# Seventy narrow warm-up products and forty one-element memsets in a hand-ordered linear-attention and MLP kernel

## The chip, the core and the metric

The kernel runs on one core of a Trainium2 chip. The metric is the device time of one execution in microseconds (us); the median of the runs is what counts. Five engines work side by side, each on its own queue, in order: TensorE (PE for its products, PEld for its weight loads), VectorE (DVE), ScalarE (ACT), GpSimd (POOL), and SyncE (SP), whose queue issues every data transfer here. Semaphores tie them together.

## The reference, cut to what matters

Sizes: 2048 rows, 512 columns, 32 heads of 16, an inner width of 1792 in the MLP; all tensors are bf16.

```python
def _layernorm(x, eps=1e-5):
    return (x - mean(x)) / sqrt(var(x) + eps)

def _A_ref(x, wqkv, wo):                      # linear attention
    q, k, v = heads(x @ wqkv)
    phi = lambda t: where(t > 0, t + 1, exp(t)) + 1e-6
    pq, pk = phi(q), phi(k)
    kv = einsum("bhsd,bhse->bhde", pk, v)
    z = einsum("bhsd->bhd", pk)
    num = einsum("bhqd,bhde->bhqe", pq, kv)
    den = einsum("bhqd,bhd->bhq", pq, z)[..., None] + 1e-6
    return merge(num / den) @ wo

def _B_ref(x, w1, w2):                        # MLP
    return maximum(x @ w1, 0) @ w2

h  = x + _A_ref(_layernorm(x), A_wqkv, A_wo)
h2 = h + _B_ref(_layernorm(h), B_w1, B_w2)
```

## The kernel before

The 2048 rows are 16 tiles of 128 rows; four tiles make a chunk. Every step is a small function `op_NAME`, and one string, `ORDER`, lists the calls: a word such as `K.3.7` calls `op_K(3, 7)`, the first number being the tile or chunk and the others banks of the accumulator `bk` (eight banks) or slices. Nothing else schedules: the order of the words is the order of the instructions on each engine, and semaphore waits are derived from the data. An engine's queue is in order, so a word that waits holds up all that stands behind it on the same engine.

The head of the program, on which the prediction rests, works tile by tile:

- `lx.t.n`, `lk`, `lq` load rows of x and the weights of k and q, on SP. `const` sets small constants on VectorE (and `zeros`, which lies in `m_sb`), and the identity on GpSimd.
- `S.t` and `A.t` (VectorE) take the statistics of a tile and join them in `mv`; `R.t.n` (ScalarE) makes `rstd` by a Ln and an Exp, two activations; `N.t` (VectorE) writes the normalised tile into `h_nat`.
- `T.t.b` transposes a tile on TensorE, in four products with the identity; `E.t` (ScalarE) copies the result to `lnT`. Later tiles go by `X.t` instead, a transposing transfer on SP.
- `K.t.b` makes the k projection, four products of 512 columns; `F`, `U`, `M`, `D` (or `W`) turn it into phi(k) on ScalarE and VectorE, in `eb` and `rb`; `G.t` adds k times x into four banks.
- `table` loads the one ScalarE table that holds both Ln and Exp. Where an activation stands in the order before a table that has its function, the build puts a table load ahead of it.
- `warm` and `warmf` are products of zeros into a bank that is not yet in use: `warm.n.b` has 512 columns of bf16, `warmf.n.b` 256 columns of f32.

Then follow the q projection (`Q`, `qF` and so on), the state `kv` and its product with `wo`, in `m_sb` (`m`), the denominators (`dn`, `dnl`, `dnx`), which are transposed into `rd` by SP (`dt`) and multiplied in by `dm` (into `pqs`), the attention output with the residual (`h`, `hD`), the second layernorm (`s`, `a`, `r`, `n`, and `x` or `t` for the transposes), and the MLP: `p` with relu in `pA` or `pD`, then `f`, `fo` and the store `fd`. The last tile's `f` comes in three pieces of 128, 256 and 128 columns.

Of the kernel before, what the change touches and what calls it, by code (L numbers as in the profile page):

```python
# [15 lines left out]


ORDER = """
const lx.0.1 lx.1.1 warmf.4.3 warm.1.3 S.0 table A.0 R.0.1 S.1 lx.2.2 lk.0.2 warm.1.3 N.0 A.1 S.2 R.1.1 lk.2.2
lx.4.2 A.2 T.0.7 E.0 warm.1.3 S.3 R.2.1 K.0.1.0.2 lx.6.2 A.3 R.3.1 K.0.1.2.2 N.1 T.1.5 F.0.1 E.1 N.2 N.3 T.3.2  # L20
lx.8.4 E.3 S.4 S.5 A.4 T.2.5 lx.12.4 lq.0.2 A.5 K.1.0.0.2 R.4.2 S.6 M.0.1 N.5 S.7 N.4 X.5 E.2 U.0.1 D.0.1 K.3.7
K.1.0.2.2 F.3.1 M.3.1 X.4 K.2.3.0.2 U.3.1 A.7 A.6 K.2.3.2.2 U.1.1 R.6.2 F.2.1 F.1.1 G.0 D.3.1 G.3 S.9 U.2.1 N.7
N.6 S.8 K.5.1 K.4.0 M.2.1 A.8 A.9 R.8.2 U.4.2 M.1.1 X.7 D.2.1 F.4.2 D.1.1 N.9 S.12 X.6 N.8 X.9 G.2 K.7.3 S.13
A.12 A.13 G.1 R.12.2 K.6.2 K.9.1 M.4.2 S.10 F.6.2 N.12 D.4.2 S.11 A.10 U.6.2 X.8 M.6.2 N.13 G.4 X.12 K.8.0 A.11
R.10.2 S.14 D.6.2 G.5 G.6 X.13 N.10 N.11 S.15 F.8.2 M.8.2 X.11 A.15 U.8.2 A.14 D.8.2 R.14.2 G.7 za.2 za.4 K.12.0
G.9 K.13.1 N.15 N.14 X.10 lq.2.2 K.11.3 F.12.2 K.10.2 M.12.2 U.12.2 F.10.2 masks X.15 X.14 lv.0.2 lv.2.2 l1.0.2
U.10.2 za.6 D.12.2 M.10.2 G.8 za.8 D.10.2 Q.0.1.1 Q.0.0.0 qF.0.0.2 qU.0.0.2 za.10 G.12 K.14.2 K.15.3 Q.0.2.0
za.12 Q.0.3.1 G.13 F.14.2 G.11 qF.0.2.2 l2.10.4 qM.0.0.2 M.14.2 W.14.2 zf.12 G.10 qD.0.0.2 qM.0.2.2 G.14
qU.0.2.2 lo.0.2 z.3.1.14 z.2.1.14 G.15 z.1.1.14 z.0.1.14 qD.0.2.2 zc gA.0.2 gA.2.2 Q.1.0.2 zh dn.0.1 Q.1.1.3
dnl.0 kv.2.7 lo.2.2 kv.1.7 kv.3.7 dnx.0.2.2 qF.1.0.2 kv.0.7 l2.3.4 dnx.0.0.2 Q.1.2.0 l1.2.2 rt.2.6 kx qM.1.0.2  # L30
Q.1.3.1 qF.1.2.2 m.0.4 m.1.5 rv.2 Q.3.1.7 qW.1.0.2 m.3.6 Q.2.3.2 dt.3 qM.1.2.2 mA.0.2 qW.1.2.2 dt.0 dt.1 m.2.5
Q.2.1.4 dn.1.0 mA.2.2 dm.0.0.2 Q.2.2.1 dm.0.2.2 dnl.1 dnx.1.2.2 h.3.6 dnx.1.0.2 h.1.5 rt.6.3 hD.3 qF.2.2.2 dt.7
s.3 re.6 h.0.0 dt.4 qU.2.2.2 hD.1 dt.5 a.3 hD.0 s.1 s.0 a.1 qM.2.2.2 a.0 Q.3.0.6 Q.2.0.3 n.3 h.2.5 n.0 dm.1.0.2
Q.3.3.1 x.3 dm.1.2.2 qF.3.0.2 hD.2 n.1 s.2 Q.3.2.0 qU.2.0.2 qF.2.0.2 h.5.2 h.6.3 a.2 qU.3.0.2 qM.2.0.2 h.4.7 n.2
qF.3.2.2 x.0 qD.2.0.2 t.2.5 qD.2.2.2 hD.4 x.1 hD.6 h.7.4 dn.2.6 hD.5 hD.7 e.2 dnl.2 qM.3.0.2 p.0.0.5 dnx.2.2.2
p.0.13.7 p.0.1.6 p.0.8.2 p.0.9.3 dnx.2.0.2 qD.3.0.2 s.4 l2.7.3 p.0.11.4 pA.0.0.2 dt.11 l2.0.3 dt.9 dt.10 r.0.4
qM.3.2.2 qW.3.2.2 s.6 dt.8 p.0.12.6 s.7 pD.0.12.2 p.0.3.1 p.0.2.0 pA.0.8.2 dn.3.2 p.0.5.7 dnl.3 p.0.4.6 a.7
dm.2.0.2 pA.0.2.2 dnx.3.0.2 dnx.3.2.2 dm.2.2.2 pD.0.4.2 h.9.0 h.8.5 p.0.6.6 p.0.7.7 dt.13 dt.12 s.5 dt.14
p.0.10.3 hD.8 dt.15 s.8 a.6 pD.0.6.2 a.4 pA.0.10.2 n.6 f.1.1.0.7 hD.9 n.7 f.1.1.7.7 s.9 dm.3.0.2 dm.3.2.2 h.11.7
a.5 n.5 h.12.2 h.15.6 h.14.4 fo.1 h.10.5 hD.11 f.0.7.0.7 hD.12 x.6 a.8 h.13.1 a.9 f.3.3.0.7 f.3.3.7.7 x.7 hD.15  # L40
n.4 hD.14 f.0.7.7.7 x.4 f.2.0.0.7 hD.13 fo.3 x.5 p.1.0.6 s.12 s.11 n.8 hD.10 fo.0 p.1.1.7 a.11 fd.0 p.1.5.3 s.10
pD.1.0.2 f.2.0.7.7 a.12 n.12 n.9 s.14 p.1.4.2 n.11 p.1.8.4 fo.2 p.1.3.1 r.4.4 a.10 a.14 p.1.13.7 p.1.2.0
pD.1.4.2 n.10 x.10 x.11 s.13 p.1.7.2 p.1.9.5 p.1.12.6 a.13 pD.1.2.2 s.15 a.15 pD.1.8.2 n.14 pD.1.12.2 p.1.6.1
n.15 x.9 x.8 pA.1.6.2 f.7.0.0.7 p.1.10.4 fd.1 p.1.11.5 pD.1.10.2 fd.3 f.5.2.0.7 p.2.9.7 p.2.11.5 f.7.0.7.7
f.5.2.7.7 fo.7 p.2.8.6 p.2.10.4 p.2.5.1 pD.2.10.2 p.2.4.0 r.8.4 pA.2.8.2 f.4.4.0.7 fo.5 p.2.2.5 fd.2 pA.2.4.2
p.2.3.6 n.13 f.4.4.7.7 p.2.1.3 x.12 p.2.0.2 f.6.0.0.7 x.14 pA.2.2.2 fo.4 x.13 x.15 p.3.3.7 p.3.7.5 p.3.2.6
r.12.4 p.3.9.4 f.6.0.7.7 pA.2.0.2 p.3.11.1 p.3.8.3 p.3.4.2 fd.4 fd.5 fo.6 pA.3.8.2 pD.3.2.2 p.3.10.0 p.3.5.3
p.3.6.4 pA.3.10.2 fd.7 pA.3.6.2 p.2.6.6 pD.3.4.2 p.2.7.7 pD.2.6.2 p.3.13.5 p.3.1.1 fd.6 p.2.12.6 p.3.0.0
p.2.13.7 f.11.3.0.7 p.3.12.4 pD.2.12.2 f.9.6.0.7 f.9.6.7.7 f.10.7.0.7 pA.3.12.2 pA.3.0.2 f.11.3.7.7 f.10.7.7.7
f.8.2.0.7 f.12.1.0.7 f.8.2.7.7 f.14.5.0.7 f.13.4.0.7 f.15.0.0.14.3.1 f.14.5.7.7 fo.11 fo.9 fo.10 fd.10 fd.11  # L50
fo.15.3.1 fo.8 f.12.1.7.7 fd.9 f.13.4.7.7 fd.8 f.15.0.0.14.0.2 fo.14 fo.12 fd.12 fo.13 fd.15.3.1 fo.15.0.2
f.15.5.0.14.2.1 fd.13 fd.14 fd.15.0.2 fo.15.2.1 fd.15.2.1
"""


# [1 line left out]
def kernel(  # L57
# [155 lines left out]
    def op_warm(n, b):
        for _ in range(n):
            nc.tensor.matmul(bk[:, b, :], lhsT=zeros[:, 0:P], rhs=zeros, start=True, stop=True)
# [376 lines left out]
```

## Time and profile before

| | |
|---|---|
| median of 3 runs | 170.3 us (169.92 to 170.45) |
| profiled execution, first to last instruction | 168.8 us |
| instructions | 2286 |
| TensorE busy | 163.1 us, 97% of the span |
| VectorE busy | 104.4 us, 62% |
| ScalarE busy | 65.1 us, 39% |
| transfers | 15.49 MB, of them 41 transposes on SP |

The page of the profile gives times of one execution. A busy share counts the time in which at least one instruction of the engine ran; products overlap in TensorE's pipeline, so a row of products is longer than their pitch, and small waits between products don't show in the share. The chain of work that ended last, in order of time, shows which engine the end waited for. A few records of products are missing from the trace; each leaves a gap of 0.05 us called "issue". Line numbers such as L310 are those of the kernel before.

### The profile page before, as it was taken

How to read it: one execution, taken by the hardware profiler on the slowest of the kernel's cores; microseconds unless marked ns; L12 is line 12 of the kernel's file. 1: busy time of each engine (PE TensorE's matmuls, PEld its weight loads, DVE VectorE, ACT ScalarE, POOL GpSimd, SP SyncE). 2: the span in 40 equal slices, each digit the busy share in tenths (PEclk: the TensorE clock that was granted, in tenths of full speed). 3: DMA queues.
4: the chain of work that ended last, by engine and by line, in shares of the span. 5: the costliest groups of instructions: out<-in, count | busy, mean ns of one | idle time of the engine just before them, and what ended most of it. 6: DMA issues, size and time to landing. Idle time of an engine off the chain costs nothing.

```text
span 168.8 us, 2286 instructions
## 1 busy us (share of the span) xinstructions
PE 163.1 (97%) x855; PEld 78.0 (46%) x871; DVE 104.4 (62%) x205; ACT 65.1 (39%) x97; POOL 4.8 (3%) x21
## 2 busy tenths in 40 slices
PE   7989999999999999999999999999999999999993
PEld 5344344445644454444444444444444444444553
DVE  3899998997668999699819879215102432050251
ACT  3698775875879947432000003004320420400000
POOL 7400000000000000000000000000000000000000
PEclk9999999999999999999999999999999999999999
DMA  4975575689533353534130015500320000002023
GB/s 112 352 245 97 97 66 124 176 270 378 174 64 65 77 138 87 134 62 95 37 62 0 31 31 122 126 4 0 62 93 0 31 0 4 0 0 93 0 65 94
DMA packets 30491, 15.49 MB, mean 92 GB/s; under 512 B 23184, under 2 KB 29328, under 8 KB 30480
## 3 DMA queue, kind: packets, MB, share of 16 engines
q1 hardware_dynamic: 30480, 15.34, 35.5%
q8 instruction: 7, 0.11, 0.3%
q14 instruction: 4, 0.03, 0.1%
HBM read 7.86 MB, written 2.10 MB: 59 GB/s over the span
## 4 chain that ended last, share of the span: by engine, by line
PE 85%; DVE 7%; DMA 4%; issue 1%; SPq 0%
PE bk L541 29%; PE bk L521 28%; PE bk L505 8%; PE bk L318 8%; PE bk L362 6%; PE bk L310 4%; DVE st L237 3%; DMA x_nat<-in_A_x_dram 2%; DMA lnT<-h_nat 2%; DVE h_nat L262 2%; PE bk L459 1%; DVE eb L335 1%; PE bk L403 1%; PE bk L415 1%; SPq L201 0%
## 5 line engine op out<-in xcount | busy, mean ns | idle before, releaser
L541 PE MATMUL bk<-w_sb,at 128*128 128x512 bf16 (+2 forms) x247 | 50.1, 355 | 0.3
L521 PE MATMUL bk<-lnT,w_sb 128*128 128x512 bf16 x219 | 50.0, 379 | 0.3
L527 ACT ACTIVATE at<-bk 128x1024 bf16<-128x1024 f32 x14 | 14.2, 1023 | 57.4 <-PE bk L521 57.4
L541 PEld LDWEIGHTS <-at 128*128 128x128 bf16 x252 | 23.6, 98 | 25.4 <-ACT at L527 0.3
L549 DVE SCALAR_TENSOR_TENSOR gT<-bk,rstd,h_nat 128x512 bf16<-128x512 f32 (+2 forms) x18 | 12.2, 689 | 35.7 <-PE bk L541 35.6
L521 PEld LDWEIGHTS <-w_sb 128*128 128x128 bf16 x224 | 21.8, 98 | 25.8
L532 DVE TENSOR_SCALAR at<-bk 128x1024 bf16<-128x1024 f32 x14 | 17.1, 1218 | 12.8 <-PE bk L521 12.6
L328 ACT ACTIVATE eb<-bk 128x1024 bf16<-128x1024 f32 (+1 forms) x18 | 16.6, 928 | 6.6 <-PE bk L310 4.8
L310 PE MATMUL bk<-wk_sb,lnT 128*128 128x512 bf16 x63 | 15.3, 380 | 0.4 <-ACT lnT L291 0.3
L505 PE MATMUL bk<-m_sb,pqs 128*128 128x512 bf16 x63 | 15.4, 380 | 0.1
L318 PE MATMUL bk<-lnT,wq_sb 128*128 128x512 bf16 x61 | 15.1, 379 | 0.1
L362 PE MATMUL bk<-at,h_nat 128*128 128x512 bf16 x55 | 13.5, 379 | 0.1
L331 ACT ACTIVATE rb<-bk 128x1024 bf16<-128x1024 f32 (+1 forms) x14 | 12.5, 904 | 0.3 <-PE bk L310 0.3
L511 DVE TENSOR_TENSOR h_nat<-bk,x_nat 128x512 bf16<-128x512 f32 x16 | 10.5, 680 | 2.9 <-PE bk L505 2.9
L237 DVE BATCH_NORM_STATS2 st<-x_nat 128x6 f32<-128x512 bf16 x16 | 10.8, 680 | 2.4 <-DMA x_nat<-in_A_x_dram 2.4
L239 DVE BATCH_NORM_STATS2 st<-h_nat 128x6 f32<-128x512 bf16 x16 | 10.7, 683 | 0.1
L310 PEld LDWEIGHTS <-lnT 128*128 128x128 bf16 x64 | 6.0, 98 | 8.4 <-ACT lnT L291 1.0
L362 PEld LDWEIGHTS <-h_nat 128*128 128x128 bf16 x64 | 6.2, 98 | 7.4 <-issue 0.2
L505 PEld LDWEIGHTS <-pqs 128*128 128x128 bf16 x64 | 5.9, 98 | 7.9 <-DVE pqs L495 1.8
L318 PEld LDWEIGHTS <-wq_sb 128*128 128x128 bf16 x64 | 5.9, 98 | 6.4
L472 ACT ACTIVATE wk_sb<-ld 128x1024 bf16<-128x1024 f32 x8 | 8.1, 1050 | 0.1
L335 DVE TENSOR_SCALAR eb<-eb 128x1024 bf16<-128x1024 bf16 (+1 forms) x18 | 6.8, 383 | 0.9 <-ACT eb L328 0.9
(63 smaller groups left out, 93.5 us busy)
## 6 DMA issues: line engine op xcount, KB each, us to landing
out_dram<-gT SPq DMA_DIRECT2D x15, 128.0 KB, 1.9
w_sb<-in_B_w_dram SPq DMA_DIRECT2D x2, 896.0 KB, 9.8
x_nat<-in_A_x_dram SPq DMA_DIRECT2D x2, 512.0 KB, 6.3
w_sb<-in_B_w_dram SPq DMA_DIRECT2D x2, 512.0 KB, 9.5
x_nat<-in_A_x_dram SPq DMA_DIRECT2D x3, 256.0 KB, 4.6
w_sb<-in_B_w_dram SPq DMA_DIRECT2D x2, 384.0 KB, 3.5
wk_sb<-in_A_wqkv_dram SPq DMA_DIRECT2D x2, 256.0 KB, 4.3
wq_sb<-in_A_wqkv_dram SPq DMA_DIRECT2D x2, 256.0 KB, 4.9
```

The lines of the kernel that those rows point to most:

```text
L237: op_S = lambda t: nc.vector.bn_stats(out=st[:, t, :], in_=x_nat[:, t, :])
L310: nc.tensor.matmul(bk[:, b, :], lhsT=lnT[c][:, kd, j * P : (j + 1) * P], rhs=wk_sb[:, kd, :], start=(kd == 0), stop=(kd == KD - 1),)
L318: nc.tensor.matmul(bk[:, b, :], lhsT=wq_sb[:, kd, j * P : (j + 1) * P], rhs=lnT[c][:, kd, :], start=(kd == 0), stop=(kd == KD - 1),)
L328: nc.scalar.activation(out=buf(eb, kind, i, n), in_=bank(at_bank[kind, i], n), func=ACT.Exp)
L331: nc.scalar.activation(out=buf(rb, kind, i, n), in_=bank(at_bank[kind, i], n), func=ACT.Relu)
L362: nc.tensor.matmul(bk[:, KD + kd, :], lhsT=ln_nat[:, t, kd * P : (kd + 1) * P], rhs=pk(t)[:, 0, :], start=(t == 0), stop=(t == NT - 1),)
L505: nc.tensor.matmul(bk[:, b, :], lhsT=pqs[:, (c * KD + jb) % NQ, j * P : (j + 1) * P], rhs=m_sb[:, jb, :], start=(jb == 0), stop=(jb == KD ...
L521: nc.tensor.matmul(bk[:, b, cols], lhsT=w1_sb[:, kd, f * P : (f + 1) * P], rhs=lnT[c][:, kd, cols], start=(kd == 0), stop=(kd == KD - 1),)
L527: nc.scalar.activation(out=acts[c % 2][:, f : f + n, :], in_=bank(at_bank["p", c, f], n), func=ACT.Relu)
L532: nc.vector.tensor_scalar(out=acts[c % 2][:, f : f + n, :], in0=bank(at_bank["p", c, f], n), scalar1=0.0, scalar2=None, op0=ALU.max,)
L541: nc.tensor.matmul(bk[:, b, 0 : w * P], lhsT=acts[c % 2][:, f, j * P : (j + 1) * P], rhs=w2_sb[:, f, k * P : (k + w) * P], start=(f == 0), ...
L549: nc.vector.scalar_tensor_tensor(out=o_t[:, t % NO, cols], in0=bk[:, at_bank["f", t, k], 0 : w * P], scalar=rstd2[:, t : t + 1], in1=h_nat ...
```

## The change

`op_warms` stood in the file unused; it is now called with 70 products of 64 columns, in place of `warmf.4.3` and beside three wide `warm` products. A new `op_idle(n)` writes n memsets of one element on VectorE, all into the same new tile `pad`: 24 of them stand between the statistics of tiles 0 and 1, and 16 between those of tiles 2 and 3. `ORDER` is written anew from its first to its last word, with other banks; all other steps are called as often as before. Two lines of it and the new code:

```diff
-const lx.0.1 lx.1.1 warmf.4.3 warm.1.3 S.0 table A.0 R.0.1 S.1 lx.2.2 lk.0.2 warm.1.3 N.0 A.1 S.2 R.1.1 lk.2.2
-lx.4.2 A.2 T.0.7 E.0 warm.1.3 S.3 R.2.1 K.0.1.0.2 lx.6.2 A.3 R.3.1 K.0.1.2.2 N.1 T.1.5 F.0.1 E.1 N.2 N.3 T.3.2
+lx.0.1 lx.1.1 lx.2.2 lk.0.2 lk.2.2 lx.4.2 lx.6.2 lx.8.4 const S.0 idle.24 S.1 A.0 R.0.1 A.1 N.0 S.2 A.2 warms.70.7
+idle.8 idle.8 S.3 A.3 warm.1.6 table R.1.1 N.1 R.2.1 R.3.1 N.2 N.3 S.4 S.5 A.4 A.5 T.0.1 warm.1.3 warm.1.4 T.1.5 T.2.3
+T.3.2 E.0 E.1 E.3 E.2 K.0.4.0.2 K.0.4.2.2 K.3.0 K.2.2.0.2 K.1.3.0.2 K.2.2.2.2 K.1.3.2.2 S.6 R.4.2 N.5 F.0.1 U.0.1
...
     eps5 = const.tile([P, 1], F32, name="eps5")
+    pad = const.tile([P, 1], F32, name="pad")
...
+    def op_idle(n):
+        for _ in range(n):
+            nc.vector.memset(pad[:], 0.0)
+
     def op_warm(n, b):
         for _ in range(n):
             nc.tensor.matmul(bk[:, b, :], lhsT=zeros[:, 0:P], rhs=zeros, start=True, stop=True)
...
     def op_warms(n, b):
         for _ in range(n):
             nc.tensor.matmul(bk[:, b, 0:64], lhsT=zeros[:, 0:P], rhs=zeros[:, 0:64], start=True, stop=True)
```

The ten loads at the head of SP's queue stand as before. The two loads of `w2` that stood among the `dt` and `x` transposes now follow the other weight loads.

What this makes of the queues is seen at two places. The first is ScalarE's queue from its start to the first copies into `lnT`. Before:

```order
L166 ACT_TABLE_LOAD
L243 ACTIVATE rstd<-mv,eps_73 128x1
L244 ACTIVATE rstd<-rstd 128x1
L243 ACTIVATE rstd<-mv,eps_73 128x1
L244 ACTIVATE rstd<-rstd 128x1
L291 ACTIVATE lnT_81<-bk 128x4x128
```

And now, with lines four further on:

```order
L247 ACT_TABLE_LOAD
L247 ACTIVATE rstd<-mv,eps_73 128x1
L248 ACT_TABLE_LOAD
L248 ACTIVATE rstd<-rstd 128x1
L166 ACT_TABLE_LOAD
L247 ACTIVATE rstd<-mv,eps_73 128x1
L248 ACTIVATE rstd<-rstd 128x1
L247 ACTIVATE rstd<-mv,eps_73 128x1
L248 ACTIVATE rstd<-rstd 128x1
L247 ACTIVATE rstd<-mv,eps_73 128x1
L248 ACTIVATE rstd<-rstd 128x1
L295 ACTIVATE lnT_82<-bk 128x4x128 x4
```

`table` (L166) has moved behind R.0, the build has put two loads of its own around R.0's Ln, and R.1 to R.3 now stand ahead of the four copies E.

The second place is VectorE's queue behind the constants, up to the fourth N (`st` and `mv` are the statistics, `h_nat` the normalised tile). Before:

```order
L237 BN_STATS st<-x_nat 128x6
L238 BN_AGGR mv<-st 128x2
L237 BN_STATS st<-x_nat 128x6
L262 TENSOR_SCALAR h_nat<-x_nat,mv,rstd 128x512
L238 BN_AGGR mv<-st 128x2
L237 BN_STATS st<-x_nat 128x6
L238 BN_AGGR mv<-st 128x2
L237 BN_STATS st<-x_nat 128x6
L238 BN_AGGR mv<-st 128x2
L262 TENSOR_SCALAR h_nat<-x_nat,mv,rstd 128x512 x3
```

And now, with the semaphores that each waits for (`DVE_49` is VectorE's own):

```order
L241 BN_STATS st<-x_nat 128x6 [waits DMAHW0_49]
L215 MEMSET pad 128x1
L215 MEMSET pad 128x1 [waits DVE_49] x23
L241 BN_STATS st<-x_nat 128x6 [waits DMAHW1_49]
L242 BN_AGGR mv<-st 128x2
L242 BN_AGGR mv<-st 128x2 [waits DVE_49]
L266 TENSOR_SCALAR h_nat<-x_nat,mv,rstd 128x512 [waits DVE_49,Activation_49]
L241 BN_STATS st<-x_nat 128x6 [waits DMAHW2_49]
L242 BN_AGGR mv<-st 128x2 [waits DVE_49]
L215 MEMSET pad 128x1
L215 MEMSET pad 128x1 [waits DVE_49] x15
L241 BN_STATS st<-x_nat 128x6
```

The joining of tile 0's statistics has moved behind the first 24 memsets and the statistics of tile 1; the other 16 memsets stand ahead of the statistics of tile 3. On TensorE the first K product now stands behind all sixteen transposes of the first four tiles; before, the K products of tile 0 stood behind four of them.

More of the change, by code (lines that the diff above doesn't have):

```diff
@@ L18 @@
 ORDER = """
-const lx.0.1 lx.1.1 warmf.4.3 warm.1.3 S.0 table A.0 R.0.1 S.1 lx.2.2 lk.0.2 warm.1.3 N.0 A.1 S.2 R.1.1 lk.2.2
-lx.4.2 A.2 T.0.7 E.0 warm.1.3 S.3 R.2.1 K.0.1.0.2 lx.6.2 A.3 R.3.1 K.0.1.2.2 N.1 T.1.5 F.0.1 E.1 N.2 N.3 T.3.2
-lx.8.4 E.3 S.4 S.5 A.4 T.2.5 lx.12.4 lq.0.2 A.5 K.1.0.0.2 R.4.2 S.6 M.0.1 N.5 S.7 N.4 X.5 E.2 U.0.1 D.0.1 K.3.7
-K.1.0.2.2 F.3.1 M.3.1 X.4 K.2.3.0.2 U.3.1 A.7 A.6 K.2.3.2.2 U.1.1 R.6.2 F.2.1 F.1.1 G.0 D.3.1 G.3 S.9 U.2.1 N.7
-N.6 S.8 K.5.1 K.4.0 M.2.1 A.8 A.9 R.8.2 U.4.2 M.1.1 X.7 D.2.1 F.4.2 D.1.1 N.9 S.12 X.6 N.8 X.9 G.2 K.7.3 S.13
@@ L24 @@
[L24 to L52, printed above, removed]
+lx.0.1 lx.1.1 lx.2.2 lk.0.2 lk.2.2 lx.4.2 lx.6.2 lx.8.4 const S.0 idle.24 S.1 A.0 R.0.1 A.1 N.0 S.2 A.2 warms.70.7
@@ new lines @@
+idle.8 idle.8 S.3 A.3 warm.1.6 table R.1.1 N.1 R.2.1 R.3.1 N.2 N.3 S.4 S.5 A.4 A.5 T.0.1 warm.1.3 warm.1.4 T.1.5 T.2.3
+T.3.2 E.0 E.1 E.3 E.2 K.0.4.0.2 K.0.4.2.2 K.3.0 K.2.2.0.2 K.1.3.0.2 K.2.2.2.2 K.1.3.2.2 S.6 R.4.2 N.5 F.0.1 U.0.1
+F.3.1 S.7 M.0.1 A.7 A.6 D.0.1 N.4 R.6.2 U.3.1 M.3.1 N.7 D.3.1 lx.12.4 lq.0.2 X.5 X.4 G.0 G.3 K.5.1 K.4.0 F.2.1 F.1.1
+U.2.1 S.8 N.6 S.9 A.8 A.9 M.1.1 M.2.1 D.2.1 R.8.2 U.1.1 F.4.2 U.4.2 N.8 N.9 S.12 D.1.1 A.12 S.13 S.14 A.13 X.7 X.6 G.2
+K.7.3 K.6.2 G.1 X.8 X.9 K.8.0 K.9.1 R.12.2 F.6.2 U.6.2 S.11 M.4.2 N.13 A.11 D.4.2 M.6.2 S.10 N.12 A.10 D.6.2 G.4 G.5
@@ new lines @@
+F.8.2 R.10.2 U.8.2 N.11 N.10 S.15 M.8.2 A.14 A.15 za.2 R.14.2 N.15 N.14 D.8.2 lq.2.2 X.13 X.12 G.7 G.6 K.13.1 K.12.0
+U.12.2 F.12.2 X.10 X.11 K.10.2 G.8 K.11.3 F.10.2 U.10.2 za.4 M.12.2 D.12.2 za.6 M.10.2 za.8 D.10.2 Q.0.0.0 Q.0.1.1
+lv.0.2 X.14 X.15 lv.2.2 l1.0.2 l2.10.4 lo.0.2 lo.2.2 l2.3.4 l1.2.2 l2.7.3 l2.0.3 masks qU.0.0.2 qF.0.0.2 G.12 K.15.3
+K.14.2 Q.0.2.0 Q.0.3.1 G.11 F.14.2 qF.0.2.2 qU.0.2.2 qM.0.0.2 za.10 M.14.2 qD.0.0.2 W.14.2 za.12 qM.0.2.2 zf.12
+qD.0.2.2 G.13 G.9 G.14 G.10 G.15 z.1.1.14 z.0.1.14 z.3.1.14 z.2.1.14 zc zh gA.0.2 gA.2.2 Q.1.0.2 dn.0.4 kv.2.5 kv.3.5
@@ new lines @@
+kv.1.5 kv.0.5 Q.1.1.3 dnl.0 dnx.0.2.2 dnx.0.0.2 qF.1.0.2 rt.2.7 Q.1.2.0 Q.1.3.1 rv.2 kx qM.1.0.2 qW.1.0.2 m.0.4 m.3.6
+m.1.5 Q.3.1.7 Q.2.3.2 qF.1.2.2 qM.1.2.2 qW.1.2.2 mA.0.2 dt.3 dt.1 dt.0 m.2.5 Q.2.1.4 dn.1.3 mA.2.2 Q.2.2.1 dm.0.0.2
+dm.0.2.2 h.1.5 hD.1 s.1 h.3.0 hD.3 a.1 dnl.1 dnx.1.0.2 h.0.6 h.2.5 Q.3.2.0 qU.2.2.2 qF.2.2.2 dnx.1.2.2 rt.6.1 re.6
+dt.5 dt.4 dt.7 hD.0 s.3 n.1 a.3 s.0 a.0 n.3 n.0 dm.1.0.2 Q.2.0.3 Q.3.0.6 Q.3.3.1 qU.2.0.2 qF.2.0.2 qU.3.0.2 qF.3.0.2
+dm.1.2.2 h.4.2 h.5.4 h.6.3 hD.2 qM.2.0.2 s.2 a.2 n.2 t.2.6 h.7.5 x.1 x.0 x.3 qF.3.2.2 e.2 p.0.10.6 p.0.11.7 pA.0.10.2
@@ new lines @@
+hD.5 hD.4 qD.2.0.2 qM.3.2.2 qM.2.2.2 hD.6 hD.7 qD.2.2.2 qM.3.0.2 qW.3.2.2 qD.3.0.2 s.5 p.0.12.4 p.0.1.3 dn.2.6 dnl.2
+dnx.2.2.2 dnx.2.0.2 r.0.4 p.0.0.2 pA.0.0.2 p.0.7.1 dn.3.7 p.0.3.6 p.0.6.0 p.0.2.5 p.0.5.3 p.0.4.2 pD.0.6.2 pA.0.2.2
+dnl.3 p.0.8.6 s.6 a.6 pD.0.4.2 a.5 dt.11 dt.8 dt.10 dt.9 dnx.3.2.2 dnx.3.0.2 p.0.13.5 p.0.9.7 pA.0.8.2 f.1.1.0.7
+f.3.3.0.7 n.5 s.4 pD.0.12.2 a.4 n.6 n.4 dm.2.0.2 dm.2.2.2 h.8.0 s.7 hD.8 a.7 f.2.2.0.7 h.10.5 hD.10 f.0.0.0.7 h.11.5
+h.9.6 f.1.1.7.7 n.7 s.8 hD.11 s.10 a.10 dt.14 dt.15 dt.13 x.6 dt.12 x.4 x.7 x.5 dm.3.0.2 dm.3.2.2 hD.9 a.8 fo.1
@@ new lines @@
+f.3.3.7.7 f.2.2.7.7 h.13.6 f.0.0.7.7 s.9 p.1.1.5 p.1.0.4 p.1.8.1 a.9 n.9 hD.13 fo.2 fo.0 s.11 fo.3 pD.1.0.2 s.13
+h.14.0 hD.14 h.12.3 p.1.9.2 p.1.2.0 n.8 hD.12 s.12 pD.1.8.2 n.10 p.1.5.7 p.1.4.6 h.15.3 pD.1.4.2 p.1.3.1 p.1.13.5
+hD.15 a.11 s.15 a.12 a.15 pD.1.2.2 p.1.12.4 p.1.6.2 p.1.11.1 p.1.7.3 fd.2 x.10 fd.1 s.14 a.14 n.11 x.11 fd.0 x.8 a.13
+n.14 x.14 n.13 n.12 n.15 pD.1.12.2 r.4.4 r.12.4 pA.1.6.2 f.5.7.0.7 p.1.10.0 pD.1.10.2 f.4.6.0.7 f.4.6.7.7 f.6.5.0.7
+f.7.1.0.7 fo.4 f.6.5.7.7 f.5.7.7.7 fo.6 fo.5 x.15 x.12 x.13 fd.4 x.9 p.2.12.2 p.2.13.3 fd.5 fd.3 p.2.7.6 p.2.11.7
@@ new lines @@
+p.2.6.5 f.7.1.7.7 pD.2.12.2 pD.2.6.2 p.3.4.2 p.3.5.3 pD.3.4.2 fo.7 fd.7 fd.6 p.3.0.0 p.2.3.4 p.2.10.6 pD.2.10.2
+p.2.2.3 p.2.4.5 p.3.1.1 p.2.5.6 p.2.9.7 pA.2.2.2 p.2.1.3 p.3.6.4 pA.2.4.2 pA.3.0.2 r.8.4 p.3.12.1 p.2.0.2 pA.2.0.2
+p.3.7.5 p.2.8.6 pA.3.6.2 p.3.3.3 pA.2.8.2 p.3.13.2 p.3.8.4 pA.3.12.2 p.3.11.7 p.3.10.6 p.3.2.2 p.3.9.5 f.8.0.0.7
+pD.3.2.2 pA.3.10.2 pA.3.8.2 f.15.3.0.14.0.2 f.11.7.0.7 f.9.2.0.7 f.14.4.0.7 f.8.0.7.7 f.12.1.0.7 f.12.1.7.7 f.9.2.7.7
+f.10.5.0.7 f.10.5.7.7 f.14.4.7.7 f.11.7.7.7 f.13.6.0.7 f.13.6.7.7 fo.8 fo.9 fo.15.0.2 fd.9 fd.8 fd.15.0.2 fo.12 fo.10
@@ L53 @@
+fo.11 fd.10 fo.14 fd.11 fd.14 fd.12 fo.13 fd.13 f.15.2.0.14.2.1 fo.15.2.1 fd.15.2.1 f.15.7.0.14.3.1 fo.15.3.1
+fd.15.3.1
 """
```

## The prediction

> **What bounds the kernel now.** I read the page first: the busy shares and the chain that ended last.
>
> ```profile
> span 168.8 us, 2286 instructions
> PE 163.1 (97%) x855; PEld 78.0 (46%) x871; DVE 104.4 (62%) x205; ACT 65.1 (39%) x97; POOL 4.8 (3%) x21
> PE 85%; DVE 7%; DMA 4%; issue 1%; SPq 0%
> ```
>
> TensorE is the bound, and 85% of the chain is its products. A busy share says little about small waits, so the chain in order of time comes next (start, length, what).
>
> ```profile
> 17.65 3.40 DMA lnT<-h_nat
> 21.10 1.04 PE bk L310 x4
> ...
> 50.35 1.97 PE bk L505 x8
> ...
> 57.73 2.16 PE bk L505 x10
> ...
> 71.70 2.00 PE bk L505 x8
> ...
> 166.16 0.03 issue
> ```
>
> From 21.10 us on the chain is TensorE alone, but for gaps of 0.05, until its last product ends at 166.16. Its pitch there is 2.16 / 10 = 0.216 us for a product of 512 columns. Two pieces are longer than their products: 1.97 and 2.00 us for eight, where 8 x 0.216 = 1.73, so 0.24 and 0.27 us of waiting. A microsecond lost before 21 us therefore comes out at the end whole, and about half a microsecond is all that could be won behind it.
>
> Third, the head: the timeline of TensorE (start, length with overlap, instruction, in brackets the wait).
>
> ```profile
> 1.24 3.78 PE L221 MATMUL bk<-m_sb 128*128 128x256 f32 x8 [1.24 <-DVE ones L177]
> 5.67 0.63 PE L281 MATMUL bk<-ident,h_nat 128*128 128x128 bf16 x4
> 6.10 0.63 PE L215 MATMUL bk<-m_sb 128*128 128x512 bf16 x1
> 6.99 1.05 PE L310 MATMUL bk<-wk_sb,lnT 128*128 128x512 bf16 x4 [0.26 <-ACT lnT L291]
> 7.87 0.90 PE L281 MATMUL bk<-ident,h_nat 128*128 128x128 bf16 x8
> 9.21 0.38 PE L281 MATMUL bk<-ident,h_nat 128*128 128x128 bf16 x4 [0.44 <-ACT lnT L291]
> 9.43 2.75 PE L310 MATMUL bk<-wk_sb,lnT 128*128 128x512 bf16 x12
> 12.13 1.02 PE L362 MATMUL bk<-pk_lo,h_nat 128*128 128x512 bf16 x4
> 19.94 1.03 PE L362 MATMUL bk<-at,h_nat 128*128 128x512 bf16 x4
> ```
>
> By 9.43 TensorE has done all sixteen transposes of the first four tiles and the four K products of tile 0; from there it streams. Two waits remain before 21.10: 12.13 - 9.43 - 12 x 0.216 = 0.11, and 21.10 - 19.94 - 4 x 0.216 = 0.30, the latter for the DMA transpose of 3.40 us in the chain. With 0.24 and 0.27 that makes 0.92 us.
>
> **The change, part by part.** The prices of the head are in the timelines of ScalarE and VectorE.
>
> ```profile
> 0.79 1.28 ACT L166 ACT_TABLE_LOAD   x1 [0.79 <-PEq L576]
> 4.06 0.30 ACT L243 ACTIVATE rstd<-mv,eps 128x1 f32<-128x1 f32 x1 [1.99 <-DVE mv L238]
> 4.39 0.20 ACT L244 ACTIVATE rstd<-rstd 128x1 f32<-128x1 f32 x1
> 6.34 0.60 ACT L291 ACTIVATE lnT<-bk 128x512 bf16<-128x512 bf16 x1 [0.64 <-PE bk L281]
> 8.57 1.08 ACT L291 ACTIVATE lnT<-bk 128x512 bf16<-128x512 bf16 x2
> 1.14 0.06 DVE L175 MEMSET eps<- 128x1 f32 x1
> 1.15 0.06 DVE L176 MEMSET eps<- 128x1 f32 x1
> 3.12 0.69 DVE L237 BATCH_NORM_STATS2 st<-x_nat 128x6 f32<-128x512 bf16 x1 [1.90 <-DMA x_nat<-in_A_x_dram]
> 3.85 0.18 DVE L238 BATCH_NORM_AGGREGATE mv<-st 128x2 f32<-128x6 f32 x1
> 4.63 0.41 DVE L262 TENSOR_SCALAR h_nat<-x_nat,mv,rstd 128x512 bf16<-128x512 bf16 x1
> 5.60 0.70 DVE L237 BATCH_NORM_STATS2 st<-x_nat 128x6 f32<-128x512 bf16 x1 [0.47 <-DMA x_nat<-in_A_x_dram]
> ```
>
> *Fillers.* The forty memsets write the same element, so each waits for the one before (the built order names that wait on 23 of the first 24). A memset of one element takes 0.06; a dependent start comes 0.04 behind the end ahead of it (3.12 + 0.69 = 3.81, then 3.85). So 0.10 each at most; I take 0.095. The other end is 0.01, the spacing of the two constants, which do not wait for each other. The dependent row is the nearer one, since it has the wait.
>
> *Table loads.* `table` now stands behind R.0, so the build puts a load of its own ahead of R.0's Ln and another ahead of its Exp, and the kernel's own load follows. The first runs under the wait for x (0.79 to 2.07) and costs nothing. The second lies between Ln and Exp of tile 0 and can't start earlier: 1.28 on the path. The third is followed.
>
> Step by step, in the new order: tile 0's statistics end at 3.81 as now, since SP's first ten loads stand as before. 24 fillers: to 6.05. S.1, now ahead of A.0: 0.65, then A.0 about 0.1: 6.75. Ln 0.30: 7.05. Second load: 8.33. Exp 0.20: 8.55; third load until 9.85. N.0 starts at 8.6, S.2 behind it ends at about 9.6, A.2 at 9.75; x of tiles 2 and 3 has been there since 5.6. Sixteen fillers, 1.5: 11.2. S.3 and A.3, 0.69 and 0.18: 12.0. ScalarE is by then through with R.1 and R.2 (9.85 + 2 x 0.53 = 10.9), so the third load is free, covered by the fillers; without them it would cost up to a microsecond. R.3 ends at 12.55. E.0 is queued behind R.3 on ScalarE and ends at 13.15; N.3 ends at 13.0 and T.3 at 13.3, ahead of the first K product in TensorE's queue. K.0 starts at 13.3 and ends at 14.15, where the old order was at 9.43. K.3 waits about 0.1 more for E.3 (two copies behind E.0, 1.08). Late by 4.8.
>
> *Warmers.* Seventy products of 64 columns: a cold one of 128 columns takes (6.10 - 5.67) / 4 = 0.107, so 70 lie between half of that, 3.7 us (start 1.24, end 5.0), and 7.5 (end 8.7). Both end before T.0's input at 9.0: no cost, hidden under the path just walked. The three wide warmers lie in the same waits. In the old order the warmers were hidden too, so nothing comes back.
>
> *Fetches.* The instruction fetches are on the page's list of queues; below it, from a window of 19 to 20.5 us, the one that runs while the transpose of 17.65 is in flight, and the landing times of the transposes into lnT and rd.
>
> ```profile
> q8 instruction: 7, 0.11, 0.3%
> q14 instruction: 4, 0.03, 0.1%
> ...
> q14 instruction: 1, 0.01, 2.3%
> ...
> DMA to landing us min/median/max: 2.4/2.5/4.1
> ...
> DMA to landing us min/median/max: 2.4/2.5/3.6
> ```
>
> Half of the transposes land within 2.5 us, the slowest take 3.6 and 4.1, and a fetch ran beside the one of 3.40. Moving the fetches can win what these late ones make TensorE wait: at most the 0.92 us counted above. The other end is nothing, since eleven or more fetches must still fall somewhere among 41 transposes. I take half, 0.45.
>
> *Everything else.* The rest of the order and the banks: the same products, evictions and transposes, so TensorE's work behind the head is the same. The two last loads of w2 move from between transposes into the burst of weight loads; they are covered by the time until the second product of the MLP, and later ones only gain slack from a late head. The tail ends as now with a piece of 128 columns and its 32 KB store. I put these at zero.
>
> Sum: 4.8 - 0.45 = +4.3, on the profiled 168.8 a span of 173.1. The profiled run is an ordinary one; the runs' median, 170.3, is 1.5 above its span, and that stays. So 174.6.
>
> **A rule on the second load.** No row shows a load behind an activation. The Trainium skill, ScalarE: Activation LUTs, What ACT_TABLE_LOAD costs, gives about 1283 ns and a drain of about 1380 ns for each switch of sets; the trace agrees on the first with 1.28 and has no drain. By it the sum would rise by an estimated 1.4 us or more.
>
> **The rivals.**
>
> 1. *The clock lapses.* Transposes at 5.67 take 0.107 each, those at 9.21 (9.43 - 9.21) / 4 = 0.055: full speed came between 6.1 and 6.99, some 5.7 us after the first warmer, though the page's clock row shows 9 throughout. In the new order the warmers end at about 5.4, then TensorE has nothing for 3.6 us, then T.0 and two warmers, then nothing for 2.4. If it is slow again at 13.3 and needs 5.7 us from T.1 at 12.4, K products run at twice 0.216 until 18.1: half of 4.8, +2.4. If it regains speed sooner, less: I take 1.7, 176.3. For it: the idle stretches. Against: the warmers came early enough to keep it partly busy. The Trainium skill, TensorE: Matmul & The Clock Gate, Part 1, has a free-running window of 3.4 us, one idle window enough to halve the clock; by it 3.6 us of idleness just suffices, in some executions only.
> 2. *A load behind an activation takes twice the row.* Second load 2.56, third to 12.4, then R.1, R.2 and R.3 in turn (3 x 0.53) and E.0: K.0 at 14.65, 176.0. For it only the lack of a row; against it that nothing in ScalarE's queue stands for a drain.
> 3. *Fillers stream.* At 0.01 each all forty cost 0.4 instead of 3.7: K.0 at about 10, 171.3. Against: their waits.
> 4. *The other side: the fetches pay.* Place: the transposes in flight at a fetch; price: 0.92. It decides only if TensorE reaches the state of 9.43 by 10.35, that is K.0 by 9.5, not 13.3; then up to 169.4. The 1.28 and the fillers' waits speak against it.
>
> That the fetches move and hit other transposes, so that the change does not do what it says, is within the first case: 175.1.
>
> **How the numbers follow.** Forecast 0.46, clock 0.33, double load 0.08, streaming fillers 0.08, fetches pay 0.05. The range goes from 172.8 (fillers at 0.06 without the gap, -1.4, and all 0.92 won, -0.45) to 177.0 (the clock's full 2.4); it leaves out the last two cases and a sum of two late mechanisms. Faster by over 0.3% (0.5 us, about what a measurement of this kernel tells from no change): 0.05. Within: 0.03. Slower: 0.92.
>
> **What the profile would show.** Right: three table loads, the second between 7.0 and 8.4; one-element memsets some 0.095 apart; the first K product near 13.3 and TensorE dense behind it; products at 14 us 0.216 apart. Clock rival: those 0.43 apart. Wrong: K.0 before 10 us, or waits of more than 1 us in TensorE behind 21 us, which I have costed at nothing new.

## The result and the profile after

The changed kernel takes 177.66 us (177.17 to 178.26, four runs) against 170.19 us for the kernel before on the same chip: a ratio of 1.044, interval 1.041 to 1.047. It is slower, as forecast, by 7.5 us where 4.3 were forecast, and outside the range.

First the page of the changed kernel: span, busy time, the share of the chain, and the granted clock in 40 slices of 4.4 us.

```profile
span 175.5 us, 2446 instructions
PE 163.4 (93%) x917; PEld 79.6 (45%) x933; DVE 107.3 (61%) x245; ACT 67.5 (38%) x99; POOL 4.7 (3%) x21
PEclk9855999999999999999999999999999999999999
PE 87%; DVE 5%; issue 2%; ACT 2%; DMA 1%; DVEq 0%
```

The busy time of TensorE is what it was. Its share fell from 97% to 93%, and the clock row has a dip in the second to fourth slice that the page of before didn't have.

The timeline of TensorE in the changed kernel's head (start, length, instruction, in brackets the wait):

```profile
1.25 3.40 PE L239 MATMUL bk<-m_sb 128*128 128x64 bf16 x70 [1.25 <-DVE m_sb L174]
9.68 0.61 PE L285 MATMUL bk<-ident,h_nat 128*128 128x128 bf16 x4 [5.04 <-DVE h_nat L266]
10.08 1.06 PE L219 MATMUL bk<-m_sb 128*128 128x512 bf16 x2
13.53 1.46 PE L285 MATMUL bk<-ident,h_nat 128*128 128x128 bf16 x12 [2.38 <-DVE h_nat L266]
14.78 4.98 PE L314 MATMUL bk<-wk_sb,lnT 128*128 128x512 bf16 x16
19.60 1.03 PE L366 MATMUL bk<-pk_lo,h_nat 128*128 128x512 bf16 x4
```

TensorE stands idle for 5.0 and 2.4 us. K.0 starts at 14.78, not at 6.99, and sixteen K products take 19.60 - 14.78 = 4.82 us, where 16 x 0.216 is 3.46. What held it up stands in VectorE's and ScalarE's timelines:

```profile
3.71 2.82 DVE L215 MEMSET pad<- 128x1 f32 x23
9.21 0.41 DVE L266 TENSOR_SCALAR h_nat<-x_nat,mv,rstd 128x512 bf16<-128x512 bf16 x1 [1.74 <-ACT rstd L248]
10.39 1.83 DVE L215 MEMSET pad<- 128x1 f32 x15
12.27 0.69 DVE L241 BATCH_NORM_STATS2 st<-x_nat 128x6 f32<-128x512 bf16 x1
7.37 0.29 ACT L247 ACTIVATE rstd<-mv,eps 128x1 f32<-128x1 f32 x1 [5.29 <-DVE mv L242]
7.68 1.28 ACT L248 ACT_TABLE_LOAD   x1
8.98 0.20 ACT L248 ACTIVATE rstd<-rstd 128x1 f32<-128x1 f32 x1
9.20 1.28 ACT L166 ACT_TABLE_LOAD   x1
13.53 0.20 ACT L248 ACTIVATE rstd<-rstd 128x1 f32<-128x1 f32 x1
```

The fillers run from 3.71 to 6.57 and from 10.39 to 12.27, the second load lies between Ln and Exp of tile 0, and the third is over at 10.48, long before R.3 ends at 13.73.

The chain in order of time, at the fillers, at the attention output's products and at the end:

```profile
3.83 0.07 DVE pad L215
3.90 0.06 issue
3.96 0.07 DVE pad L215
...
57.52 3.45 PE bk L509 x16
...
162.46 10.38 PE bk L545 x68
172.86 0.35 DVE gT L553
```

A filler starts every 0.126 to 0.13 us. At 57.52, sixteen products take 3.45, which is 16 x 0.216: the waits that made eight of them 1.97 and 2.00 us before are gone. TensorE's stream behind the head holds less than 0.1 us of waiting, where it held 0.92. The last product ends at 172.86 instead of 166.18, 6.7 us later, which is the difference of the spans.

Last, the granted clock, from a table of stretches (length, busy time and count of each engine, granted clock, share of the DMA engines, GB/s):

```profile
0.00:3.80 3.80, 2.55 (x48) 2.55 (x49) 1.00 (x6) 1.28 (x1) 2.72 (x14) 1.00 0.47 118
3.90:7.20 3.30, 0.74 (x24) 0.65 (x22) 1.87 (x24) 0.00 (x0) 1.91 (x7) 1.00 0.92 297
7.40:17.40 10.00, 5.34 (x25) 2.76 (x26) 6.81 (x32) 7.59 (x18) 0.00 (x0) 0.50 0.36 139
17.60:21.00 3.40, 3.40 (x17) 1.57 (x16) 3.12 (x11) 3.11 (x8) 0.00 (x0) 1.00 0.34 77
```

The clock is at half from about 7.3 to 17.5 us. In the first of these rows it is shown as 1.00, though warmers run at half speed there: 48 starts in the 2.55 us from 1.25 to 3.80, 0.053 each, as 64 columns take at half speed. The clock column starts to mean something at its first change.

### The profile page after: what moved, and what is told of

Its sections match the earlier page's. It is cut to its first block, busy times and chain, and to the rows that moved or that the text cites. A ratio compares the mean times of both kernels' runs of the same rounds, so it can differ in the third digit from the quotient of the medians.

```text
span 175.5 us, 2446 instructions
## 1 busy us (share of the span) xinstructions
PE 163.4 (93%) x917; PEld 79.6 (45%) x933; DVE 107.3 (61%) x245; ACT 67.5 (38%) x99; POOL 4.7 (3%) x21
## 4 chain that ended last, share of the span: by engine, by line
PE 87%; DVE 5%; issue 2%; ACT 2%; DMA 1%; DVEq 0%
PE bk L525 28%; PE bk L545 27%; PE bk L322 8%; PE bk L509 8%; PE bk L366 7%; PE bk L314 7%; DVE st L241 2%; DVE pad L215 1%; DMA x_nat<-in_A_x_dram 1%; PE bk L285 1%; PE bk L463 1%; DVE h_nat L266 1%; ACT L248 1%; PE bk L407 1%; PE bk L419 0%
## 5 line engine op out<-in xcount | busy, mean ns | idle before, releaser
L545 PE MATMUL bk<-w_sb,at 128*128 128x512 bf16 (+2 forms) x246 | 49.2, 355 | 0.3
L247 ACT ACTIVATE rstd<-mv,eps 128x2 f32<-128x2 f32 (+2 forms) x14 | 4.1, 292 | 35.5 <-DVE mv L244 26.3
L314 PE MATMUL bk<-wk_sb,lnT 128*128 128x512 bf16 x62 | 16.1, 405 | 0.1
L366 PE MATMUL bk<-at,h_nat 128*128 128x512 bf16 x55 | 13.0, 379 | 0.1
L335 ACT ACTIVATE rb<-bk 128x1024 bf16<-128x1024 f32 (+1 forms) x14 | 12.4, 896 | 1.6 <-PE bk L314 1.3
L241 DVE BATCH_NORM_STATS2 st<-x_nat 128x6 f32<-128x512 bf16 x16 | 10.7, 680 | 1.9 <-DMA x_nat<-in_A_x_dram 1.8
L314 PEld LDWEIGHTS <-lnT 128*128 128x128 bf16 x64 | 6.6, 104 | 8.3 <-issue 1.8
L285 PE MATMUL bk<-ident,h_nat 128*128 128x128 bf16 x16 | 2.1, 309 | 7.4 <-DVE h_nat L266 7.4
```

Source lines behind the costliest of these rows:

```text
L241: op_S = lambda t: nc.vector.bn_stats(out=st[:, t, :], in_=x_nat[:, t, :])
L314: nc.tensor.matmul(bk[:, b, :], lhsT=lnT[c][:, kd, j * P : (j + 1) * P], rhs=wk_sb[:, kd, :], start=(kd == 0), stop=(kd == KD - 1),)
L335: nc.scalar.activation(out=buf(rb, kind, i, n), in_=bank(at_bank[kind, i], n), func=ACT.Relu)
L366: nc.tensor.matmul(bk[:, KD + kd, :], lhsT=ln_nat[:, t, kd * P : (kd + 1) * P], rhs=pk(t)[:, 0, :], start=(t == 0), stop=(t == NT - 1),)
L545: nc.tensor.matmul(bk[:, b, 0 : w * P], lhsT=acts[c % 2][:, f, j * P : (j + 1) * P], rhs=w2_sb[:, f, k * P : (k + w) * P], start=(f == 0), ...
```

## The experiments

The theory, from the profile after: the loss is all in the head, the sum of fillers that wait for each other, of the second table load, and of the half clock; behind the head the moved fetches win something. The rivals: one of the three is covered by another; or the new order costs time behind the head; or the fetches do nothing. In the diffs below, lines of `ORDER` are cut to the words that change. Differences from the changed kernel are between medians; its four runs span 1.1 us and were measured apart from those below, so such a difference is known to about half a microsecond, and the times of one profile, such as the start of K.0, are the sharper evidence.

### Each part of the head taken away from the changed kernel

Fillers that do not wait for each other, at the same places and in the same number:

```diff
-    pad = const.tile([P, 1], F32, name="pad")
+    pad = const.tile([P, 40], F32, name="pad")
...
-            nc.vector.memset(pad[:], 0.0)
+            nc.vector.memset(pad[:, i : i + 1], 0.0)     # i counts the forty
```

> The changed kernel, but each of the forty memsets writes an element of its own, so none waits for another; the number of instructions on every engine is unchanged, and with it where the fetches fall. Fillers theory (the waits between the memsets hold up the head: 24 and 16 steps of 0.126 us, 5.0 us, of which some 0.4 stays): first K product at about 10.3 instead of 14.8 and, TensorE being idle for less than 2.5 us at a time, the clock not halved: 171.4 us (171.0 to 172.5). If the clock is halved again: 172.5 to 174. Rival (the fillers are covered, the loss is in the table loads, the clock or the new order): above 176.

173.22 us (172.76 to 173.58), ratio to before 1.018 (1.016 to 1.021): 4.4 us less than the changed kernel. From the timelines of VectorE and TensorE:

```profile
3.64 0.34 DVE L218 MEMSET pad<- 128x1 f32 x23
1.25 3.92 PE L242 MATMUL bk<-m_sb 128*128 128x64 bf16 x70 [1.25 <-DVE ones L177]
10.49 5.38 PE L317 MATMUL bk<-wk_sb,lnT 128*128 128x512 bf16 x16
15.71 1.03 PE L369 MATMUL bk<-pk_lo,h_nat 128*128 128x512 bf16 x4
```

Twenty-three fillers take 0.34 us instead of 2.82, and K.0 starts at 10.49. The fillers are the larger part of the loss. The time lies in the second of the ranges expected, but the clock was not halved again: in this execution it had not risen before. The seventy warmers take 3.92 us, at 0.053 each, where they took 3.40 in the changed kernel, and the sixteen K products take 15.71 - 10.49 = 5.22 instead of 3.46, so half speed lasted from the start to about 14.0. The mean granted clock of this run reads 0.998 all the same, because the record begins with its first change.

One table load ahead of S.0:

```diff
-lx.8.4 const S.0 idle.24 ... warm.1.6 table R.1.1
+lx.8.4 const table S.0 idle.24 ... warm.1.6 R.1.1
```

> The changed kernel, but `table` is the last word ahead of S.0, so there is one table load, under the wait for x. Table theory: 1.28 us off the path between tile 0's statistics and its first normalised tile, nothing else: 176.3 us, the first K product at 13.5, if the clock is halved as before; 174.5 to 175.3 if the shorter gap in TensorE leaves the clock at full speed. Rival (loads are covered by the fillers): 177.4 to 177.9.

176.50 us (176.16 to 177.11), 1.2 us less than the changed kernel; K.0 at 13.40.

```profile
13.40 5.04 PE L314 MATMUL bk<-wk_sb,lnT 128*128 128x512 bf16 x16
```

The second load is on the path and the third is not. Both edits together:

> Both edits: fillers that do not wait, and `table` ahead of S.0. Theory of the head (all of the loss is the late start of TensorE, by fillers, loads and the halved clock they cause): first K product at about 9, and 169.5 to 170.6 us, as before the change. Rival (the new order, its banks or the places of the fetches cost time behind the head): 171 to 174. Rival (the new places of the fetches pay): below 169.6.

171.84 us (170.94 to 172.35), ratio 1.010 (1.006 to 1.014), 5.8 us less: the two add (4.4 + 1.2 = 5.6). It is above what the theory of the head gave, and in the range of its first rival, but not by that rival's cause: K.0 starts at 9.68, and the clock is at half until about 12.2. The clock is taken away further below.

The clock, first with sixteen more f32 warmers:

```diff
-S.3 A.3 warm.1.6 table ... T.0.1 warm.1.3 warm.1.4 T.1.5
+S.3 A.3 warm.1.6 warmf.10.6 table ... T.0.1 warm.1.3 warm.1.4 warmf.6.3 T.1.5
```

> The changed kernel with sixteen more wide f32 warmers in TensorE's two idle stretches (ten ahead of T.0, six ahead of T.1), nothing else touched. Clock theory: the products of 14.8 to 17.5 us run at 0.216 instead of 0.427, part of it taken back by VectorE and ScalarE behind them: 175.9 us (175.4 to 176.4), first K product at 14.4. Rival (the clock is beside the point, the chain runs over ScalarE and VectorE there): 177.3 to 178.

176.97 us (176.82 to 178.15): the full clock is there, half of the gain or more is not. The chain shows where it went in the profiled run, which is the slowest of the four, 178.15:

```profile
33.96 4.27 DMA lnT<-h_nat
38.23 0.05 issue
38.27 1.90 PE bk L314 x8
```

A transpose landed after 4.27 us and TensorE waited for it, 0.85 us until 38.27; another wait, of 1.04, ended at 58.09. The other three runs took 176.82 to 177.08, so they hold these waits at most in part. The 64 more instructions on TensorE had moved its fetches: one now starts at 35.79, while this transpose is in flight. So the clock was tried again with the number of instructions kept:

```diff
-            nc.tensor.matmul(bk[:, b, 0:64], lhsT=zeros[:, 0:P], rhs=zeros[:, 0:64], start=True, stop=True)
+            nc.tensor.matmul(bk[:, b, 0:w], lhsT=zeros[:, 0:P], rhs=zeros[:, 0:w], start=True, stop=True)
...
-warms.70.7 ... T.0.1 warm.1.3 warm.1.4 T.1.5
+warms.48.7.256 ... T.0.1 warm.1.3 warm.1.4 warms.22.3.256 T.1.5
```

> The changed kernel with its seventy warmers made 256 columns wide and split, 48 ahead of T.0 and 22 between T.0 and T.1: TensorE has work almost all the time, and as many instructions as before on every engine, so the fetches stay where they are. Clock theory: full speed from about 7 us on, the K products at 0.216 from 14.4: 1.2 to 1.3 us less than the changed kernel, 176.4 us (175.9 to 176.9). Rival (the half clock is covered by ScalarE and VectorE): 177.3 to 178.

176.29 us (176.01 to 176.60), 1.4 less than the changed kernel. The same table of stretches:

```profile
10.00:14.00 4.00, 3.38 (x33) 2.55 (x30) 2.94 (x23) 2.12 (x8) 0.00 (x0) 1.00 0.26 95
14.00:21.00 7.00, 6.84 (x37) 3.04 (x35) 6.96 (x23) 6.12 (x16) 0.00 (x0) 1.00 0.21 48
```

The half clock cost 1.4 us by the medians. In the profiles it is 1.2 (175.5 against 174.3): the sixteen K products end 1.6 us earlier, and then TensorE waits 0.32 us at 19.2 for VectorE's phi(k), a wait that the half clock had hidden. All three parts taken away at once (`warms.44.7.128` ahead of T.0, `warms.26.3.128` behind it):

> Fillers that do not wait and `table` ahead of S.0, and the seventy warmers 128 columns wide and split, 44 ahead of T.0 and 26 between T.0 and T.1; instruction counts unchanged. Clock theory: no half clock after 8 us, the first K product at 9.1 and at full speed: 170.4 us (169.9 to 170.9). Rival (the order behind the head costs the rest): 171.3 to 172.

170.77 us (170.67 to 171.80), ratio 1.004 (1.002 to 1.006). Fillers, loads and clock are 6.9 of the 7.5 us. The remaining 0.6 was not taken apart further; in this profile K.0 stands behind sixteen transposes still and ends 0.4 us later than in the kernel before, and TensorE waits 0.32 us until 13.76 for VectorE's phi(k).

### Whether the fetches matter

More narrow warmers in the changed kernel, which end well ahead of T.0, so that only TensorE's fetches and the moment of the clock's fall move:

```diff
-warms.70.7
+warms.102.7
```

> The changed kernel with 102 narrow warmers instead of 70: they end at about 6.5, still under the wait for T.0, but every later fetch of TensorE comes 64 instructions earlier in the program. Fetch theory: the fetches of about 37 and 56 us meet transposes that TensorE is about to need, as where wide warmers were added (waits of 0.85 and 1.04 us there): 179.4 us (178.5 to 180.2), with two waits of that size. Rival (those waits came from the earlier full clock, not from the fetches): 177.2 to 178.2, no wait above 0.3 us behind the head.

178.66 us (177.83 to 179.84), 1.0 more than the changed kernel: one of the two waits expected came, the other did not. The queue row is from the window 34.5 to 38.5 us, the wait from 36 to 42, the rest from the chain:

```profile
q8 instruction: 1, 0.02, 2.0%
...
PEld L314 <- DMA lnT<-h_nat: 1.2, 1, 1.2
...
35.05 4.30 DMA lnT<-h_nat
39.35 0.04 issue
39.40 1.90 PE bk L314 x8
```

In the changed kernel no fetch runs in that window, the transpose issued at 35.1 lands in 2.37 us, and TensorE does not wait. The medians alone do not decide, since the runs overlap (177.17 to 178.26 for the changed kernel). The trace does: here the wait is 0.88 us, and the last product ends 0.82 later than in the changed kernel's profile. The rival (no wait above 0.3 us) is refuted by a change of 64 instructions whose own run time is covered; in the run with f32 warmers, with as many instructions more on TensorE, the wait stood at the same product.

The same from the other side, in the kernel before, with forty free fillers where VectorE waits for x:

```diff
-lx.0.1 lx.1.1 warmf.4.3 warm.1.3 S.0 table
+lx.0.1 lx.1.1 warmf.4.3 warm.1.3 idle.40 S.0 table     # op_idle as in the first experiment
```

> The kernel before with forty fillers that don't wait ahead of S.0, where VectorE waits for x: only the two fetches of VectorE (19.5 and 84.1 us) move, 40 instructions earlier. Fetch theory: the transpose issued at 17.65 lands in 2.5 us instead of 3.4 and the wait of 0.30 at 20.6 is gone, 169.9 us (169.6 to 170.0). Rival (the fetch meets earlier transposes instead and costs as much there): 170.1 to 170.5.

169.59 us (169.22 to 169.97, ten runs), ratio 0.997 (0.995 to 0.998): faster than both kernels, by 0.4 us against the kernel before. Its chain, at the place where before the transpose of 17.65 took 3.40 us:

```profile
18.35 1.73 PE bk L315 x8
20.08 0.86 PE bk L367 x4
20.94 0.86 PE bk L315 x4
```

20.08 + 0.86 = 20.94: no wait, and that transpose now lands in 2.42 us. VectorE's fetch has moved from 19.5 to 10.7. In this profile the wait at 71 is gone too, 0.28 us; no fetch of VectorE stood there, and TensorE's instruction count is unchanged, so that part is not shown to be the edit's doing.

TensorE's fetches alone, in the kernel before:

```diff
-warmf.4.3
+warms.70.3
```

> The kernel before with the seventy narrow warmers in place of the four f32 ones: only TensorE's fetches move, some 120 instructions earlier. Fetch theory: the waits of TensorE near 50 and 71 us move or go; 169.8 to 170.6 us, by where the fetches near 35 and 55 us fall. Rival (fetches don't matter): every wait stays where it was, 170.0 to 170.3.

171.30 us (170.85 to 171.40), ratio 1.006 (1.005 to 1.008): slower, and above the range. The fetch that now starts at 52.1 meets two transposes into `rd`, which take 3.72 and 3.08 us; TensorE waits 0.32 at 57 and 0.34 at 80, while the waits at 50 and 71 are gone. The one of 0.30 at 20.6, beside VectorE's fetch, stayed. With 0.15 more at 60 to 62 their net is 0.3 of the 0.4 us between the two profiles (spans of 168.8 and 169.2). The medians differ by 1.3; most of that loss is not located.

> The kernel before with both: narrow warmers and free fillers, its own order kept. If the effects of the two moves of fetches add: the sum of the two single runs against the kernel before, 169.5 to 170.5 us. If the changed kernel's order is needed beside them, none below 170.0.

171.26 us (170.35 to 171.69), ratio 1.006 (1.004 to 1.009). The two moves do not add up to the sum of the single ones (0.9 over before, where 1.2 was measured). In the profiled run the load of x for tiles 4 and 5 landed 1.6 us later than before and VectorE waited for it; why is open. The wait of 0.30 at 20.6 is gone in this profile too, as in the one with free fillers alone.

### The head, from the kernel before and in the new order

One table load turned into three, in the kernel before:

```diff
-S.0 table A.0 R.0.1 S.1
+S.0 A.0 R.0.1 table S.1
```

> The kernel before, with `table` moved behind R.0 and nothing else: three table loads instead of one. Table theory: the second load, 1.28 us, is on the path to N.0, and the third, 1.28 more, on the path to R.1, since no fillers cover it here; K.0 follows E.0, which stands behind R.1: K.0 at about 8.3 to 9.5 instead of 7.0, 171.3 to 172.5 us. Rival (the later waits of TensorE in the head take it back): 170.0 to 170.6.

172.18 us (171.31 to 172.34), ratio 1.011 (1.008 to 1.014). From the timelines of ScalarE and TensorE:

```profile
4.65 1.28 ACT L244 ACT_TABLE_LOAD   x1
6.17 1.28 ACT L166 ACT_TABLE_LOAD   x1
8.53 1.89 PE L310 MATMUL bk<-wk_sb,lnT 128*128 128x512 bf16 x4 [1.26 <-ACT lnT L291]
```

Without fillers to cover it the third load is on the path too, and a half clock came with TensorE's waits here as well (8.1 to 11.5 us).

The old head in front of the new order, with one table load and free fillers ahead of S.0:

```diff
-const S.0 idle.24 S.1 A.0 R.0.1 A.1 N.0 S.2 A.2 warms.70.7 idle.8 idle.8 S.3 A.3 warm.1.6 table R.1.1 ...
+const table idle.24 idle.8 idle.8 S.0 A.0 R.0.1 S.1 warms.70.7 warm.1.6 N.0 A.1 S.2 R.1.1 A.2 T.0.1 E.0 warm.1.3
+warm.1.4 S.3 R.2.1 K.0.4.0.2 A.3 R.3.1 K.0.4.2.2 N.1 T.1.5 E.1 N.2 N.3 T.3.2 S.4 E.3 S.5 A.4 A.5 T.2.3 E.2 ...
```

> The changed kernel's order from the first S.6 on, with the words of the old head in front (A.0 and R.0 ahead of S.1, T.0, E.0 and K.0 ahead of the other transposes), `table` first, all forty fillers ahead of S.0 and not waiting for each other, the warmers as changed; the counts of instructions on TensorE, VectorE and SP as in the changed kernel. Theory (the head alone lost the time, and the new order with its fetches leaves no waits behind it): K.0 at about 7, no wait of TensorE behind 12 us above 0.2: 169.3 us (168.9 to 169.8), below the kernel before. Rival (the waits are gone only because the late head gave the other engines a lead): 170.0 to 171.5, with waits back between 12 and 75 us.

170.35 us (170.13 to 171.25, twelve runs), ratio 1.000 (0.998 to 1.002). My theory was wrong here, and the rival right in its time: waits came back, 0.32 at 12.4, where TensorE waits for VectorE's phi(k), and 0.60 at 57, the latter in the chain:

```profile
54.19 2.43 DMA rd<-wk_sb
...
56.74 0.70 DVE pqs L502
57.45 0.05 issue
57.49 2.94 PE bk L512 x12
```

The transpose took an ordinary 2.43 us; it was issued late. The reason stands on SP's queue. This is the group of three transposes to which it belongs, here and, below, in the changed kernel:

```profile
50.72 4.68 SPq L498 DMA_TRANSPOSE rd<-wk_sb  x3
...
58.16 4.03 SPq L495 DMA_TRANSPOSE rd<-wk_sb  x3
```

The first of the three kept SP for 2.06 us here, where the others took 1.2 each, and a fetch of TensorE ran from 51.01 to 52.35; the two behind it were issued that much later. In five other runs of this order a fetch also ran beside the first transpose of this group, and the wait grew with the time that it kept SP: where that one kept SP for 1.41 us (the changed kernel), TensorE does not wait; at 1.53 and 1.54 (all three parts taken away, and fillers alone) it waits 0.09; at 1.70 (both edits, and table alone) 0.25; at 2.06 it waits 0.60. So this wait goes with a fetch and not with the missing lead. What the lead, and with it the half clock, had hidden is the 0.32 for phi(k): it stands in all four profiles of this order in which the K products ran at full speed from the first, and in none of the others.

## Why the prediction was right and wrong

- *The bound* held: a loss in the head came out at the end whole.
- *The path* held link by link: fillers, S.1, Ln, second load, Exp, N.0, S.2, fillers, S.3, N.1 to N.3, T.3, K.0; R.3 and E.0 ended ahead of T.3, as in my walk. The third load was free, as said, and the experiment without waiting fillers in the old order shows that it is on the path where nothing covers it.
- *The second load* was right at 1.28 with 0.02 behind it to the Exp (7.68 + 1.28 = 8.96, then 8.98); taking it away gave 1.2. Rival 2, a load of twice the row, falls by these rows. The drain that the Trainium skill names (ScalarE: Activation LUTs, What ACT_TABLE_LOAD costs) does not show here.
- *The fillers were mis-sized*: I took 0.095 each, they took 0.126. On the path the two rows took 4.65 us (3.75 to 6.57 and 10.44 to 12.27), where my walk has 3.69, so 1.0 us was missing. K.0 came 1.5 later than forecast; of the rest 0.3 is the half-speed transposes, and about 0.1 is A.0, for which I wrote 0.1 though its row says 0.18. The waiting row I used was right in kind; it was a wait behind an instruction of 0.7 us, and behind one of 0.06 the step is longer than the sum.
- *The clock was put in the wrong place*: it was a rival at 0.33 and should have stood in the sum. The idle stretches I had worked out myself, 3.6 and 2.4 us, were 5.0 and 2.4. Its price was 1.4 by experiment, against 1.7 taken. The 5.7 us that I let it take to come back were one execution's: here full speed came 2.6 us after the first warmer and, later, 4.0 us after work resumed. That the first warmers brought full speed at 3.9 did not help; they ended at 4.65 and speed fell at 7.3. The Trainium skill, TensorE: Matmul & The Clock Gate, Part 1, gives a window of 3.4 us; the trace agrees, with full speed for 3.4 us and half for 10.2, three times as long.
- *The fetches*: of the 0.92 us of waits less than 0.1 is left, where I took half by a guess. In the profile of before 0.81 of the 0.92 stand behind a fetch: the 0.30 behind the transpose of 3.40 us, and the 0.24 and 0.27 behind transposes that kept SP for 1.76 and 1.69 us during the fetches of 47.2 and 63.6. Shown by moving a fetch alone is the 0.30; the rest is read from the traces.
- *The warmers and the fourth rival*: no cost in their own time, as said; the fetches paid, but far below the head's loss.

On the profiled runs: K.0 ends at 14.78 + 4 x 0.427 = 16.49 instead of 9.43, 7.06 late (4.8 forecast, K.3's wait included); half speed until 17.54 adds (17.54 - 16.49) / 2 = 0.52; the waits give back 0.85 or a little more. That makes 6.7, what was measured. The range failed since its upper end held the clock alone with the fillers at my price; the two came together.

## What to carry to other kernels

An instruction put in to shift something costs by the wait it carries, not by its length: forty memsets to one element cost 4.4 us, to forty elements next to nothing. Where TensorE streams, long gaps ahead of the stream have a second price, the half clock after them: it came with two idle stretches of 1.2 us or more (both edits, and the three table loads in the kernel before), and not with gaps of up to 0.8. So size the gaps first and put the clock in the sum. A transfer that stands alone on the path can be late because an instruction fetch runs beside it; count instructions per engine when a kernel is edited, and move such a fetch with free instructions that stand under a wait. Then measure: one such move won 0.4 us here, and another, of TensorE's fetches, lost 1.3.
